# Attention of batches three to eight in quarters of TensorE's array, with a new layout of the PSUM banks

## The chip, the core and the metric

One core of a Trainium2 chip runs the whole program. TensorE (PE) multiplies and writes its products to PSUM, eight banks of 512 fp32 columns on 128 partitions; VectorE (DVE), ScalarE (ACT) and GpSimd (POOL) do the elementwise work, SyncE (SP) issues nearly all DMAs. PE keeps one operand in the array (a weight load, PEld in the profile) and streams the other through it, column by column. The metric is the device time of one execution in microseconds.

## What is computed

Eight batches of eight heads, 576 positions, 64 numbers per head. The first four heads attend to the last 32 positions ("plain"), the other four to every fourth of the last 128 ("dilated"). The heads' outputs, side by side, are the 512 columns of 4608 tokens, which go through a feed-forward of width 2048 with a leaky ReLU. Inputs and output are fp32, the kernel works in fp16.

```python
scores = scale * np.matmul(q, k.transpose(0, 1, 3, 2))
mask_plain = (rel >= 0) & (rel < window)                                       # window = 32
mask_dil = (rel >= 0) & (rel < window * dilation) & (rel % dilation == 0)      # dilation = 4
scores = np.where(masks[None, :, :, :], scores, -1000000000.0)
attn = np.exp(scores - np.max(scores, axis=-1, keepdims=True))
attn = attn / (np.sum(attn, axis=-1, keepdims=True) + 1e-09)
attn_out = np.matmul(attn, v)
x = attn_out.transpose(0, 2, 1, 3).reshape(B * S, H * D)
h = x @ w_in
return np.maximum(0.01 * h, h) @ w_out
```

## The kernel before

**Attention.** A visit is one pair of heads of one batch, four visits a batch in the order `VISITS` (2 and 3 dilated, 0 and 1 plain). `load_qk`, `load_v` and `load_rest` stage fp32 rows, `cast` turns them into fp16, `turn` puts Q and K of the pair into a slot with the 64 numbers of each head on partitions. For batches 0 and 1 (`b < EARLY`, `by_pe`) PE transposes; for batches 2 to 7 the load itself scatters 32-row pieces of 128 bytes (L437) and DVE transposes 32 by 32 (L708 to L720), with copies by POOL and ACT for the dilated order and for K, in which the keys of the two heads interleave, so that a full 128-row array holds 64 keys of each.

`unit` does half the queries of a visit: five score matmuls (L899) into one bank, Exp on ACT (L907), the product with a 0/1 table on DVE (L911; batches 0 and 1 add a bias on PE instead), row sums with a matrix of ones (L924), values (L918) into a second bank, Ln and Exp(−x) on ACT (L943, L945) for the reciprocal, and the product into `xt` on DVE (L956). For the plain visits from batch 2 on (`ADDED`; the 9 for the dilated ones means never) DVE or POOL first adds overlapping pieces of the weights (L932), which shortens the sums on PE.

**Feed-forward.** Twelve chunks of 384 tokens, three for two batches. `up` (L1057) multiplies `xt` by `w_in`, 16 blocks of four matmuls of 384 columns, and ACT applies the leaky ReLU into `gt` (L1073); chunk 1 is done in halves (`up_pair`, L1091). The last three chunks use seven products instead of eight (`ups7`, L1191). `down` (L1271) and `group` (L1361, seven products for four tiles) multiply by `w_out`; ACT and DVE evict, SP stores.

**What sets the order.** Every piece of work is a task of `_Plan` with its engine, a duration that the planner assumes, and what it waits for. `_Plan.run` makes a list schedule eight times and takes the best; the table `NUDGE` then shifts the priority of single tasks by their number, `HAND` fixes the engine of some, and the plan is made once more. The instructions of each engine stand in that order for good. `WHEN` gives the due time of each batch's attention. Before the feed-forward starts, spare time of PE is filled with matmuls on zeros (L1475, L1601).

**Banks.** Eight separate tiles: `tp`, `ops` twice, `hps` twice (for `up`), `sps`, `fps` twice. Units use `sps` and `ops`; `group` uses `fps` and `tp`.

## Time and profile before

| | us |
|---|---|
| three runs | 293.78, 294.69, 296.07 |
| median | 294.69 |
| span of the profiled execution, first to last instruction | 292.5 |

The profiled execution's own time is not listed apart from its span; the median lies 2.2 us above the span. The engines' times in 40 equal slices of the span, in tenths, with the granted clock of TensorE and the DMA share:

```profile
PE   6899999999999999999999999999999999999995
PEld 2567776776787788677777877887688999999985
DVE  7877588674799789858839889897878889678672
ACT  3997987589869966878888987888767966755522
POOL 5420452458537746964873774653425000000000
PEclk9999999999999999999999999999999999999999
DMA  7999999799898959999799798751101210121133
```

Attention of the last batch ends in slice 33 (235 us); behind it only the last chunks are left. The page's groups by line stand with the prediction, where they are used.

### The profile page before, as it was taken

What the parts mean: (1) busy time and instruction counts of PE and PEld (TensorE: products, weight loads), DVE (VectorE), ACT (ScalarE), POOL (GpSimd) and SP (SyncE); (2) the same over time, 40 slices, a digit from 0 to 9 for tenths busy, and PEclk for the clock granted to TensorE, in tenths of its full rate; (3) what the DMA queues carried; (4) which work ended last, traced back from release to release, by engine and by line L of the source; (5) the groups of instructions that cost most, each with busy time, mean ns of one, the idle gap of its engine ahead of it and who ended that gap; (6) DMA issues with size and microseconds to landing.
All of it is one profiled execution on the core that took longest, in us unless ns stands there. A gap on an engine that the chain in (4) does not pass through costs nothing.

```text
span 292.5 us, 7626 instructions
## 1 busy us (share of the span) xinstructions
PE 285.2 (97%) x2924; PEld 226.4 (77%) x2924; DVE 226.8 (78%) x437; ACT 218.9 (75%) x483; POOL 121.2 (41%) x173
## 2 busy tenths in 40 slices
PE   6899999999999999999999999999999999999995
PEld 2567776776787788677777877887688999999985
DVE  7877588674799789858839889897878889678672
ACT  3997987589869966878888987888767966755522
POOL 5420452458537746964873774653425000000000
PEclk9999999999999999999999999999999999999999
DMA  7999999799898959999799798751101210121133
GB/s 244 267 389 396 395 377 224 150 168 218 142 188 185 179 144 174 191 168 208 197 170 160 180 205 151 195 134 59 36 2 36 75 38 0 38 74 36 38 109 110
DMA packets 156068, 47.15 MB, mean 161 GB/s; under 512 B 136832, under 2 KB 153344, under 8 KB 156032
## 3 DMA queue, kind: packets, MB, share of 16 engines
q1 hardware_dynamic: 155344, 46.04, 65.0%
q10 hardware_dynamic: 688, 0.63, 0.6%
q8 instruction: 23, 0.38, 0.5%
q14 instruction: 13, 0.11, 0.1%
HBM read 37.22 MB, written 9.44 MB: 160 GB/s over the span
## 4 chain that ended last, share of the span: by engine, by line
PE 93%; ACT 2%; DVE 2%; DMA 1%; issue 1%; ACTq 0%; DVEq 0%
PE hps L1057 27%; PE fps L1361 23%; PE tp L1361 9%; PE hps L1191 5%; PE fps L1271 4%; PE hps L1091 4%; PE ops L1191 3%; PE ops L918 3%; PE ops L899 2%; PE sps L899 2%; PE ops L924 2%; PE sps L1191 1%; DMA con<-consts 1%; PE sps L924 1%; PE ops L1361 1%; PE sps L918 1%
## 5 line engine op out<-in xcount | busy, mean ns | idle before, releaser
L1057 PE MATMUL hps<-xt,w_in 128*128 128x384 f16 x488 | 94.7, 325 | 0.0
L1361 PEld LDWEIGHTS <-gt 128*128 128x128 f16 x768 | 73.0, 98 | 9.8 <-DVE gt L1347 0.2
L1073 ACT ACTIVATE gt<-hps 128x384 f16<-128x384 f32 x122 | 59.1, 487 | 13.7 <-PE hps L1057 12.7
L1057 PEld LDWEIGHTS <-w_in 128*128 128x128 f16 x512 | 44.9, 98 | 21.3 <-issue 0.3
L505 POOL CAST slots<-vst 128x576 f16<-128x576 f32 x55 | 46.0, 861 | 22.7 <-DMA vst<-in_v_dram 5.6
L505 POOL CAST nat<-stg 128x576 f16<-128x576 f32 (+1 forms) x52 | 34.6, 687 | 48.6 <-DVE gt L1347 15.1
L1361 PE MATMUL fps<-w_out,gt 128*128 128x256 f16 x368 | 46.7, 272 | 0.0
L911 DVE TENSOR_TENSOR ee<-ee,con 128x384 f16<-128x384 f16 (+1 forms) x48 | 20.6, 430 | 15.3 <-ACT ee L907 14.9
L945 ACT ACTIVATE rc<-rc 128x288 f32<-128x288 f32 (+1 forms) x64 | 27.2, 436 | 1.1
L956 DVE TENSOR_TENSOR xt<-ops,rc 128x288 f16<-128x288 f32 (+2 forms) x44 | 19.3, 445 | 9.7 <-ACT rc L945 4.9
L516 ACT COPY slots<-turned 64x512 f16<-64x512 f16 (+1 forms) x30 | 23.8, 799 | 0.8 <-DVE turned L708 0.5
L1214 ACT ACTIVATE gt<-vst 128x384 f16<-128x384 f32 (+1 forms) x24 | 16.0, 684 | 8.0 <-DVE vst L1210 8.0
L899 PEld LDWEIGHTS <-slots 128*128 128x128 f16 x308 | 18.1, 98 | 4.7 <-DVE slots L517 0.4
L517 POOL COPY slots<-turned 64x576 f16<-64x576 f16 (+2 forms) x25 | 16.7, 675 | 11.2 <-ACT slots L516 3.5
L907 ACT ACTIVATE ee<-ops 128x416 f16<-128x416 f32 (+2 forms) x35 | 16.7, 487 | 3.6 <-PE ops L899 3.0
L918 PEld LDWEIGHTS <-slots 128*128 128x128 f16 x308 | 17.1, 97 | 2.8 <-ACT slots L504 0.6
L924 PEld LDWEIGHTS <-con 128*128 128x128 f16 x168 | 14.0, 97 | 5.9 <-issue 0.8
L708 DVE STREAM_TRANSPOSE turned<-nat 128x576 f16<-128x576 f16 x24 | 18.0, 759 | 0.1
L1390 ACT COPY stg<-fps 128x512 f32<-128x512 f32 (+1 forms) x20 | 10.4, 519 | 9.4 <-PE fps L1361 9.1
L907 ACT ACTIVATE ee<-sps 128x416 f16<-128x416 f32 (+2 forms) x29 | 14.4, 495 | 3.8 <-PE sps L899 2.7
L1347 DVE TENSOR_TENSOR gt<-gt 128x1024 f16<-128x1024 f16 x21 | 16.6, 789 | 0.3 <-PE fps L1361 0.2
L1191 PEld LDWEIGHTS <-w_in 128*128 128x128 f16 x192 | 16.2, 98 | 0.2
(158 smaller groups left out, 559.8 us busy)
## 6 DMA issues: line engine op xcount, KB each, us to landing
out_dram<-osb SPq DMA_DIRECT2D x32, 256.0 KB, 2.6
stg<-in_k_dram SPq DMA_DIRECT2D x48, 144.0 KB, 3.6
stg<-in_q_dram SPq DMA_DIRECT2D x48, 144.0 KB, 3.4
vst<-in_v_dram SPq DMA_DIRECT2D x16, 288.0 KB, 4.3
vst<-in_v_dram SPq DMA_DIRECT2D x32, 128.0 KB, 3.2
gt<-in_moe_w_in_dram SPq DMA_DIRECT2D x6, 512.0 KB, 6.8
stg<-in_q_dram SPq DMA_DIRECT2D x3, 512.0 KB, 6.9
stg<-in_k_dram SPq DMA_DIRECT2D x3, 512.0 KB, 9.1
```

Of the source, the lines that this page charges most:

```text
L505: return ENG[e].tensor_copy(out=dst, in_=src)
L516: return nc.scalar.copy(out=dst, in_=src)
L899: nc.tensor.matmul(p_bank[:, c:c + w], slot(tn, KB + 128 * s, 0, 128, [1, 128]), slot(tn, qx, 0, 128, *qd), start=first or not by_pe, stop ...
L907: lambda e: nc.scalar.activation(out=et[:, 0:n], in_=p_bank[:, 0:n], func=AF.Exp, scale=SCALE), prio)
L911: lambda e: nc.vector.tensor_tensor(out=et[:, 0:n], in0=et[:, 0:n], in1=con[:, table:table + n], op=ALU.mult), prio,
L918: nc.tensor.matmul(at(dst, 0, 128, o, *od), lhs(s), et[:, c:c + w], start=i == 0, stop=i == len(steps) - 1, skip_group_check=True)
L924: nc.tensor.matmul(at(p_bank, 0, 128, o, *od), block_ones, at(et, 0, 128, c, *cd), start=i == 0, stop=i == len(rows) - 1, skip_group_check ...
L945: lambda e: nc.scalar.activation(out=rt, in_=rt, func=AF.Exp, scale=-1.0), prio)
L1057: nc.tensor.matmul(ht[:, 0:n], at(w_in, 0, 128, vi * DFF + j // 2 * 256 + j % 2, [2, 128]), at(xt[m % 2], 0, 128, vi * 1152 + x0 + x, [1, n]),
L1073: lambda e: nc.scalar.activation(out=gt[c % NG][:, j * n_c + x:j * n_c + x + n], in_=ht[:, 0:n], func=AF.Prelu, alpha=0.01),
L1191: nc.tensor.matmul(bk[:, n * i:n * i + n], w(v, 2 * z + i), x(v), start=first and i == 0 and v == 0, stop=i == 1 and v == 1, skip_group_ch ...
L1361: nc.tensor.matmul(bk[:, x:x + HN], tl[:, off + j * step:off + j * step + 128], rhs(j), start=first and x == 0 and j == 0, stop=j == HJ - ...
```

## The change

It rewrites the attention of batches 2 to 7; batches 0 and 1 and the feed-forward keep their arithmetic.

- **Quarters.** A visit is done in one burst (`burst`). Each matmul has 64 rows and 64 columns of the array (`tile_position`): the row half p holds one half of the keys, the column half q one head. Scores: five blocks for each p and q, 20 matmuls. Sums (with a 64-column block of ones) 20, values 24 (plain) or 28 (dilated). A burst has the sums and values of an earlier visit (`now`) and the scores of the next one (`then`): 26 bursts, 24 of them with scores and 24 with sums and values. The row halves write different banks; a burst holds four banks, `lent` (the one of `fps0`, `fps1`, `tp32` that `group` uses last), `sps`, `ops0`, `ops1`, or, where `fps1` is lent, `ops1`, `ops0`, `fps1`, `sps`.
- **Banks in one tile** `psum`, in the order tp, fps0, ops0, sps, ops1, fps1, hps0, hps1. One instruction of ACT or DVE reads two banks that lie side by side: Exp of 2 × 448 or 2 × 384 columns, Ln of 2 × 288, the product into `xt`. Where the two are not neighbours (`far`), it stays two instructions.
- **Masks.** The bias on PE stays for batches 0 and 1. The table has 640 columns and a block of ones, in all 704 constants behind the bias instead of 1,600. The added overlaps (`ADDED`, `LAPS`) are gone.
- **Q, K, V.** For batches 3 to 7 DVE transposes straight into the slot; only the dilated order needs one more copy (POOL or ACT) for each of Q and K. Batch 2 (`b < PACKED`) is loaded in rows of 1 KB and transposed by PE, as batches 0 and 1. V from batch 2 on is loaded per head, in pieces of 512 or 256 bytes, and cast once a visit. The columns of V and the rows of `w_in` are laid out head after head, also for batches 0 and 1.
- **Order.** `place` sets a burst after every 4.65 blocks of `up` from the 20.5th on, which ends attention with chunk 8. `FIRST`, `NUDGE` and `HAND` are new throughout.

```diff
-WHEN = (3.92, 2.82, 39.64, 80.18, 115.4, 117.81, 161.72, 152.03)
+WHEN = (3.92, 2.82)
+PLACE = 20.5
+PACE = 4.65
+SWITCH = 0.3
...
-ADDED = (2, 9)
-LAPS = ("DVE", "POOL")
...
-    EARLY = 2
+    EARLY, PACKED = 2, 3
...
-    ee = [sbuf(f"ee{i}", [128, 544]) for i in range(NE)]
-    rc = [sbuf(f"rc{i}", [128, 320], FP32) for i in range(NR)]
+    e_all = sbuf("ee", [128, 896 * NV])
+    ee = [e_all[:, 544 * i:544 * i + 544] for i in range(NE)]
+    r_all = sbuf("rc", [128, 1152], FP32)
+    rc = [r_all[:, 320 * i:320 * i + 320] for i in range(NR)]
...
-    tpb = bank("tp", FP16)
-    tp32 = tpb.bitcast(FP32)
-    ops = [bank(f"ops{i}") for i in range(2)]
-    hps = [bank(f"hps{i}") for i in range(2)]
-    sps = bank("sps0")
-    fps = [bank(f"fps{i}") for i in range(2)]
+    psum = ps.tile([128, 4096], FP32, name="psum")
+    tp32, fps0, ops0, sps, ops1, fps1, hps0, hps1 = (psum[:, 512 * i:512 * i + 512] for i in range(8))
+    tpb, hps, fps, ops = tp32.bitcast(FP16), [hps0, hps1], [fps0, fps1], [ops0, ops1]
...
-        early, first = b < EARLY, b == 0
+        early, first = b < PACKED, b == 0
...
+        if b >= PACKED:
             got = []
+            for o, x in ((0, 0), (1, KB)):
+                if not dil:
+                    got.append(add("DVE", 0.72, [c_qk[o]] + old,
+                                   lambda e, o=o, x=x: nc.vector.transpose(
+                                       slot(tn, x, 0, 128, [1, S]), na[:, o * S:o * S + S]), prio))
+                    n_users.append(got[-1])
+                    continue
...
+        if b >= EARLY:
+            got = []
+            for o in range(2):
+                if not dil:
+                    dst = slot(tn, KB * o, 0, 128, [4, 128], [1, 4])
+                    src = at(bq, 0, 128, 512 * o, [1, 128], [128, 4])
+                else:
+                    dst = slot(tn, KB * o, 0, 128, [128 if o else 144, 4], [1, 128])
+                    src = at(bq, 0, 128, 512 * o, [128, 4], [1, 128])
+                got.append(move(dst, src, 512, after_q + old, prio, ("DVE", "ACT"), dil, bank_q))
...
-        t_m = t_e if by_pe else add(
-            "DVE", 0.08 + n * 0.00052, [t_e, t_con[0]],
-            lambda e: nc.vector.tensor_tensor(out=et[:, 0:n], in0=et[:, 0:n],
-                                              in1=con[:, table:table + n], op=ALU.mult), prio,
-            lock=True)
-
...
-        if added:
-            c0, d0, c1, d1, w = lap
...
+    def places(b, vi):
+
+        if vi < 2:
+            order = [(4, 0, 64)] + [(i, 64 + 96 * i, 96) for i in range(4)]
+            return [(i, c, w, [([1, 64], 64 * (i + 4 * p)) for p in range(2)],
+                     [([[1, w]], 64 * (i + 4 * p)) for p in range(2)]) for i, c, w in order]
+        got = []
...
+    def quarter(rows, cols):
+        return 64 * rows, 64 * rows + 64, 64 * cols, 64 * cols + 64
...
+    def burst(now, then, prio, lent):
+
+        seats = [ops1, ops0, fps1, sps] if lent is fps1 else [lent, sps, ops0, ops1]
+        room, mine, far = {}, {}, seats[2].offset - seats[0].offset > 512
+        for bk in seats:
+            room[key(bk)], mine[key(bk)] = grab(bk)
...
+        def product(bk, x, od, lhs, rhs, p, q, first, last):
+            p0, p1, q0, q1 = quarter(p, q)
+            jobs.append(lambda: nc.tensor.matmul(
+                at(bk, q0, q1, x, *od), lhs(p0, p1, q), rhs(p0, p1), start=first, stop=last,
+                skip_group_check=True, tile_position=(p0, q0)))
...
+            for n, two in enumerate(list(zip(sums_of(vi, 0), sums_of(vi, 1)))
+                                    + list(zip(values_of(vi, 0), values_of(vi, 1)))):
+                for p, (blk, c, w, dims, x, *part) in enumerate(two):
+                    if not part:
...
+        if then is not None:
+            b2, v2, en2, e_old, e2_users = then
+            t2 = slot_of[b2, v2]
+            for _, c, w, keys, asks in places(b2, v2):
+                for p in range(2):
...
+        t_b = add("PE", SWITCH + cols / 2400.0, deps, pe, prio, 0.0, "B")
...
+            t_l = add("ACT", 0.07 + S / 1200.0, [t_b] + r_old,
+                      lambda e: nc.scalar.activation(out=at(rt, 0, 128, 0, [288, 2], [1, 288]),
+                                                     in_=bass.AP(
+                                                         tensor=psum.tensor, offset=seats[1].offset + 224,
+                                                         ap=[list(psum.ap[0]), [
+                                                             seats[3].offset - seats[1].offset, 2], [1, 288]]),
+                                                     func=AF.Ln), prio)
+            t_r = add("ACT", 0.105 + S / 1200.0, [t_l],
+                      lambda e: nc.scalar.activation(out=rt, in_=rt, func=AF.Exp, scale=-1.0), prio)
...
+            for i, n0, n1 in ((0, 0, 32), (1, 32, 144)) if vi >= 2 else ((0, 0, 64), (1, 64, 288)):
+                w = n1 - n0
+                for p, np in [(0, 1), (1, 1)] if far and not i else [(0, 2)]:
...
+        for p, np in [(0, 1), (1, 1)] if far else [(0, 2)]:
...
+            done.append(add("ACT", 0.07 + np * n / 1200.0, [t_b] + e_old,
+                            lambda e, p=p, np=np, part=part: nc.scalar.activation(
+                                out=at(et, 0, 128, 448 * p, [448, np], [1, n]), in_=part,
+                                func=AF.Exp, scale=SCALE), prio))
...
+        t_m = add("DVE", 0.08 + 2 * n * 0.00052, done + [t_con[0]],
+                  lambda e: nc.vector.tensor_tensor(
+                      out=at(et, 0, 128, 0, [448, 2], [1, n]), in0=at(et, 0, 128, 0, [448, 2], [1, n]),
+                      in1=at(con, 0, 128, table, [0, 2], [1, n]), op=ALU.mult), prio, lock=True)
...
+    pairs, due = [], []
+    for b, vi in [(b, vi) for b in range(EARLY, B) for vi in VISITS] + [(B, None)] * 2:
+        pairs.append((due.pop(0) if due else None, (b, vi) if b < B else None))
+        if b < PACKED:
+            due.append((b, vi))
+        elif b < B and vi % 2:
+            due += [(b, vi - 1), (b, vi)]
...
+    def place(k):
+        return PLACE + PACE * k
+
+    def bursts(upto, prio):
+        while flow[0] < len(pairs) and place(flow[0]) <= upto:
+            now, then = pairs[flow[0]]
+            if then is not None:
+                b, vi = then
...
+            burst(now, then, prio, lent[0])
...
+            if c > 1:
+                bursts(n_up[0], begins[c] + j * 1.3)
...
-        if e >= EARLY:
-            fetch(e, WHEN[e], (WHEN[e + 1] - WHEN[e]) / 4)
-        attend(e, WHEN[e], (WHEN[e + 1] - WHEN[e]) / 4 if e else 1.0)
-        if m:
-            fetch(o, WHEN[o], 6.5)
...
+        for c, batches in ((3 * m, [e]), (3 * m + 1, [e, o]), (3 * m + 2, [o])):
+            if c in SEVEN:
+                if c == SEVEN[0]:
+                    bursts(1e9, begins[c])
+                    in_sums()
```

On PE, before: the five scores of one unit of a dilated visit, between two blocks of `up` (`hps` are up's banks, `ops` a unit's, `slots` Q and K).

```order
L1057 MATMUL hps_102<-xt_86,w_in 128x384
L899 LDWEIGHTS slots
L899 MATMUL ops_101<-slots 128x96
L899 LDWEIGHTS slots
L899 MATMUL ops_101<-slots 128x96
L899 LDWEIGHTS slots
L899 MATMUL ops_101<-slots 128x80
L899 LDWEIGHTS slots
L899 MATMUL ops_101<-slots 128x80
L899 LDWEIGHTS slots
L899 MATMUL ops_101<-slots 128x32
L1057 LDWEIGHTS w_in
```

On PE now: the middle of a burst, where the sums (`con` holds the ones, `ee` the weights) give way to the values (`slots` holds V).

```order
L1260 LDWEIGHTS con
L1260 MATMUL psum<-ee,con 64x32
L1260 LDWEIGHTS con
L1260 MATMUL psum<-ee,con 64x64
L1260 LDWEIGHTS con
L1260 MATMUL psum<-ee,con 64x64
L1260 LDWEIGHTS slots
L1260 MATMUL psum<-ee,slots 64x64
```

Scores, sums and values of a unit stood in three places among the feed-forward's blocks; now all 64 or 68 matmuls of a burst stand in one, 64 rows wide, each with its weight load.

On SP, before: the loads of batch 2 behind the constants (`stg` stages Q and K, `vst` V).

```order
L489 DMA con<-consts 128x1600
L489 DMA stg_65<-in_k_dram 32x36x32 x3
L489 DMA stg_64<-in_q_dram 32x36x32 x3
L489 DMA stg_65<-in_k_dram 32x36x32
L489 DMA stg_64<-in_q_dram 32x36x32
L489 DMA vst_73<-in_v_dram 64x2x64
```

On SP now, at the same place:

```order
L659 DMA con<-consts 128x704
L659 DMA stg_68<-in_q_dram 64x8x64
L659 DMA stg_68<-in_k_dram 64x8x64
L659 DMA stg_65<-in_k_dram 128x4x256
L659 DMA vst_73<-in_v_dram 64x4x128 x3
L659 DMA vst_74<-in_v_dram 64x5x64 x3
L659 DMA stg_64<-in_q_dram 128x4x256
```

Batch 2's K and Q come in one load for four heads where eight loads of 32 × 36 pieces stood, V in more loads.

On ACT, before: one visit's Exp, Ln and Exp(−x), among the leaky ReLUs of `up` (L1073).

```order
L907 ACTIVATE ee_81<-sps_104 128x384
L1073 ACTIVATE gt_90<-hps_103 128x384
L1073 ACTIVATE gt_90<-hps_102 128x384
L907 ACTIVATE ee_82<-ops_101 128x384
L1073 ACTIVATE gt_90<-hps_103 128x384
L943 ACTIVATE rc_83<-sps_104 128x288
L1073 ACTIVATE gt_90<-hps_102 128x384
L945 ACTIVATE rc_83<-rc_83 128x288
```

On ACT now (L1405 is up's leaky ReLU):

```order
L1318 ACTIVATE rc<-psum 128x576
L1359 ACTIVATE ee<-psum 128x896
L1405 ACTIVATE gt_80<-psum 128x384 x2
L1325 ACTIVATE rc<-rc 128x576
L1405 ACTIVATE gt_80<-psum 128x384 x2
L1359 ACTIVATE ee<-psum 128x896
```

Three instructions a visit took the place of six, each about twice as wide.

439 lines of the change are left out of this document (273 added, 166 removed), and 311 rows, old and new, of the table NUDGE.

## The prediction

> **What bounds the kernel now.** I read the page's busy line and its chain of waits first, then a table of stretches, then the order of time on PE.
>
> ```profile
> span 292.5 us, 7626 instructions
> PE 285.2 (97%) x2924; PEld 226.4 (77%) x2924; DVE 226.8 (78%) x437; ACT 218.9 (75%) x483; POOL 121.2 (41%) x173
> ...
> PE 93%; ACT 2%; DVE 2%; DMA 1%; issue 1%; ACTq 0%; DVEq 0%
> ```
>
> TensorE is busy for 97% of the span and carries 93% of the chain that ends last. A busy PE could still hide holes, so the next view cuts the span into stretches (length, busy time of each engine, granted clock, DMA share, GB/s).
>
> ```profile
> 0.00:24.00 24.00, 19.96 (x214) 12.43 (x215) 19.09 (x37) 17.57 (x40) 9.04 (x18) 1.00 0.94 308
> 24.00:60.00 36.00, 35.70 (x383) 26.27 (x380) 26.17 (x55) 28.28 (x66) 12.62 (x18) 1.00 0.99 298
> 60.00:100.00 40.00, 39.95 (x389) 29.71 (x388) 30.66 (x59) 34.24 (x75) 25.95 (x38) 1.00 0.94 182
> 100.00:150.00 50.00, 50.00 (x497) 38.56 (x495) 37.98 (x76) 39.11 (x89) 34.54 (x50) 1.00 0.88 177
> 150.00:200.00 50.00, 50.00 (x511) 39.33 (x510) 43.62 (x81) 42.52 (x95) 28.24 (x40) 1.00 0.82 170
> 200.00:235.00 35.00, 35.00 (x378) 29.20 (x377) 27.56 (x52) 27.02 (x64) 10.79 (x11) 1.00 0.09 32
> 235.00:290.00 55.00, 54.55 (x567) 50.85 (x563) 41.72 (x82) 30.11 (x60) 0.00 (x0) 1.00 0.16 54
> ```
>
> From 24 to 235 us PE is idle for 0.35 us in all, at full clock. So in the stretch that the change touches (batches three to eight, numbered 2 to 7 in the code, from about 64 to 235 us) the time is the sum of what PE streams. What ACT, DVE and POOL save there is worth nothing by itself. What counts is how long PE needs for attention before and after, and whether a new wait appears. The second tight resource is DMA, with a share of 0.82 to 0.99 up to 200 us.
>
> **What is removed from PE.** The order of time on PE shows three kinds of attention groups between the blocks of the feed-forward: scores (L899), sums (L924) and values (L918). The columns are start, length and what ran; a length holds the drain of the last matmul, which overlaps the next row. The cost of a group is therefore the start of the next row minus its own start.
>
> ```profile
> 117.32 0.34 PE L899 MATMUL ops<-slots 128*128 128x96 f16 x5
> 117.50 0.81 PE L1057 MATMUL hps<-xt,w_in 128*128 128x384 f16 x4
> ...
> 119.02 0.34 PE L918 MATMUL sps<-ee,slots 128*128 128x96 f16 x5
> 119.21 1.46 PE L1057 MATMUL hps<-xt,w_in 128*128 128x384 f16 x8
> 120.50 0.33 PE L924 MATMUL ops<-ee,con 128*128 128x192 f16 x3
> 120.69 1.46 PE L1057 MATMUL hps<-xt,w_in 128*128 128x384 f16 x8
> ...
> 131.24 0.35 PE L899 MATMUL ops<-slots 128*128 128x96 f16 x5
> 131.44 1.46 PE L1057 MATMUL hps<-xt,w_in 128*128 128x384 f16 x8
> 132.74 0.35 PE L899 MATMUL sps<-slots 128*128 128x64 f16 x5
> 132.92 0.81 PE L1057 MATMUL hps<-xt,w_in 128*128 128x384 f16 x4
> ...
> 135.09 0.30 PE L924 MATMUL ops<-ee,con 128*128 128x32 f16 x3
> 135.23 0.65 PE L1057 MATMUL hps<-xt,w_in 128*128 128x384 f16 x3
> ```
>
> The six groups cost 0.18, 0.19, 0.19, 0.20, 0.18 and 0.14 us, on average 0.18. Six batches times four visits times two units are 48 units of three groups: 144 × 0.18 = **25.9 us removed**.
>
> **What is added to PE.** First, batch 2 is now transposed by PE as batches 0 and 1 are: four visits of eight transposes and four for the rest, 36 in all.
>
> ```profile
> 8.94 0.39 PE L791 MATMUL fps<-con,rest 128*128 128x128 f16 x4
> 9.16 0.22 PE L743 MATMUL fps<-con,nat 128*128 128x128 f16 x1
> ```
>
> Four cost 9.16 − 8.94 = 0.22, so 36 cost **2.0 us**.
>
> Second, the 26 bursts: 24 visits with scores and 24 with sums and values, in all 1,584 matmuls of 64 rows by 64 columns, each with a weight load of its own, where 612 full ones stood. No row shows a matmul in a quarter, so I bound it. The price of a full one follows from these rows (the third, from the chain of waits, is 16 matmuls of 192 columns):
>
> ```profile
> 21.74 0.53 PE L997 MATMUL sps<-slots 128*128 128x16 f16 x14
> 22.11 0.30 PE L924 MATMUL ops<-ee,con 128*128 128x192 f16 x3
> ...
> 27.26 1.32 PE hps L1091 x16
> ```
>
> A matmul of 192 columns costs 1.32/16 = 82.5 ns, one of 384 costs 1.29/8 = 161 ns (119.21 to 120.50), so about 0.41 ns a column and 3 ns a matmul; one of 16 columns costs 0.37/14 = 26 ns, a floor under the short ones, weight load included.
>
> Lower end: the four quarters run at once. Each streams 1,216 columns a visit (1,280 plain, 1,152 dilated) in 16.5 matmuls: 1,216 × 0.41 + 16.5 × 3 ns = 0.55 us, plus about four short ones raised to 26 ns (0.04), so 0.59 us × 24 = **14.2 us**, 9 ns a pair. Upper end: every pair waits its turn at the floor of 26 ns, 1,584 × 26 = 41.2 us. I take the lower end: the rows' cost runs with the columns streamed, and four quarters stream apart from each other.
>
> The page "TensorEngine Tiling (Array Packing)" of the Trainium skill, section Key Properties, says that different tiles load weights and multiply in parallel; no run here shows it yet.
>
> Third, the change of shape at a burst's two ends. No row shows one. The nearest is the drain that every group shows: the eight matmuls at 119.21 last 1.46 us, until 120.67, while the next begin at 120.50, so 0.17 us of each block drains under its successor. If shapes can't overlap, each of the 52 ends costs up to 0.17 us, 8.8 us in all; if they can, nothing. With no row nearer to either I take the middle, one drain a burst: 26 × 0.17 = **4.4 us**. The same section of that skill page says that changing the tiling mode drains the engine; by that the sum would take the full 8.8 us, and the time would be 293.8.
>
> **What is moved beside PE.** ACT and DVE work on both heads of a visit at once.
>
> ```profile
> L945 ACT ACTIVATE rc<-rc 128x288 f32<-128x288 f32 x48 | 20.7, 442 | 0.9
> L907 ACT ACTIVATE ee<-ops 128x384 f16<-128x384 f32 (+1 forms) x26 | 12.8, 502 | 3.3 <-PE ops L899 2.7 <-DVE turned L713 0.6
> L943 ACT ACTIVATE rc<-ops 128x288 f32<-128x288 f32 x26 | 10.4, 409 | 3.1 <-PE ops L924 3.1
> ```
>
> ACT gave a visit 2 × (502 + 409 + 442) = 2.71 us. With the slope between L943's 288 columns and L907's mean of 400 (about 0.85 ns a column) one Exp of 896 takes an estimated 0.92 us and the 576-wide Ln and Exp 0.65 and 0.69: 2.26 us, 0.45 less, 11 us over 24 visits. DVE loses one of two mask products, the added rows of L932 and the turned copies, POOL and ACT most copies out of them. All of it lies beside PE (hidden, worth 0); if that cover went, PE's own 0.35 us of idle time is all that it could have cost before.
>
> A burst waits once, for four banks, its masked weights, V and the next visit's Q and K; behind it on PE stands the whole feed-forward. The bursts stand some 3 to 13 us of PE work apart, and the chain from a burst's scores to the next one's weights is one Exp and one mask product, so I cost that wait at 0.
>
> DMA: batch 2's Q and K leave the 32-row, 128-byte pattern for 1 KB pieces; the constants shrink from 1,600 to 704 columns; V is cut into more pieces. The start (Q of group 0 first on SP, POOL's casts in another order) has 4.0 us of PE idle in its 24; I take no change there, give or take 1 us.
>
> **The sum.** −25.9 + 2.0 + 14.2 + 4.4 = −5.3 us. The profile's span, 292.5, lies 2.2 below the runs' median of 294.69, and that difference stays: **289.4 us**. Without any drain it is 285.0, with both drains 293.8.
>
> **The rivals.**
>
> *Quarters take turns* (slower). The whole gain hangs on one number: with drains as above the 1,584 pairs must cost less than (25.9 − 2.0 − 4.4)/1,584 = 12.3 ns each, about half the floor of 26. Two at a time: 28.4 instead of 14.2, 303.6 us. All in turn: 41.2, 316.4 us. For it speaks that no pair in the trace is faster than 26 ns; against it, that those all use the same full array.
>
> *Quarters' weights come too slowly* (no change). The loads' records here take 98 ns for 128 columns:
>
> ```profile
> L918 PEld LDWEIGHTS <-slots 128*128 128x128 f16 x308 | 17.1, 97 | 2.8 <-ACT slots L504 0.6 <-issue 0.5
> ```
>
> If half the columns took half of it, 49 ns, and the four loads of a step ran side by side without the next step's overlapping, 396 steps would cost 19.4 us instead of 14.2: 294.6 us. The skill's page "TensorE: Matmul & The Clock Gate", section LDWEIGHTS (loading the stationary operand), gives columns/1.2 ns, 53 ns for 64 (for 128 it gives 107, where the rows have 98), and the tiling page's Restrictions say that column tiling turns the fast weight load off; by these the time would be an estimated 296.2.
>
> *Both drains and a weight load unhidden at each end.* 52 × (0.17 + up to 0.098) us: 293.8 to 298.9 us.
>
> *DMA comes too late.* The new order pulls attention forward: the instructions ahead of batch 4's first scores in the two programs, counted at the prices above, come to some 106 us of PE work before and 90 now. They began here:
>
> ```profile
> 115.84 0.34 PE L899 MATMUL ops<-slots 128*128 128x96 f16 x5
> ```
>
> With DMA at 0.94 before that, data must come up to 16 us sooner; batch 2's relief (some 14,000 packets fewer for that batch, V's smaller pieces counted) gives only part of it. If 3 to 8 us stay uncovered: 292.4 to 297.4 us.
>
> **How the numbers follow.** A measurement of this kernel can tell about 1% from no change, 2.9 us. Four quarters at once with drains between none and both: 0.62 (0.50 below 291.7 us, 0.12 within 1%). Slow weights: 0.07, within. Unhidden ends: 0.08 (0.03 within, 0.05 slower). Late DMA: 0.07 (0.04 within, 0.03 slower). Two at a time: 0.09, slower; all in turn: 0.07, slower. So faster 0.50, same 0.26, slower 0.24. The range runs from 285.0 (no drain) to 299.0 (unhidden ends) and leaves out the turns, 0.16; the likeliest case's own is 285.0 to 293.8.
>
> **What would show it.** In the new profile the 64-wide matmuls must start 9 to 10 ns apart within a burst and a visit's burst must cost 0.6 us plus its ends; the gap from the last matmul before a burst to its first, and after it, gives the drain. PE must stay at 50.00 of 50.00 us in the middle stretches. Starts 13 ns or more apart, PE idle before L1260 released by DMA or POOL, or an evict of hps stuck behind the 896-wide Exp would make the prediction wrong.

## The result: slower, 307.2 us against 294.6

| | before | after |
|---|---|---|
| median, us | 294.55 | 307.16 |
| lowest, highest (four runs each) | 293.78, 296.07 | 306.08, 311.2 |
| span of the profiled execution | 292.5 | 304.7 |

The ratio is 1.0411, 95% interval 1.0364 to 1.0458. The forecast was 289.4 us, in a range of 285.0 to 299.0. One execution of the changed kernel, 311.2 us, fell into a slower state and is not in the ratio; the median of its other three, 306.5 us, is what the experiments are compared with.

The page of the changed kernel: span, PE's busy time, the main DMA queue (packets, MB, share of 16 engines' span) and the chain that ended last.

```profile
span 304.7 us, 9438 instructions
PE 285.9 (94%) x3929; PEld 219.7 (72%) x3929; DVE 212.2 (70%) x386; ACT 197.7 (65%) x401; POOL 90.1 (30%) x124
...
q1 hardware_dynamic: 146608, 46.60, 62.9%
...
PE 33%; DMA 26%; SPq 22%; DVE 7%; issue 5%; POOL 3%; ACT 3%; POOLq 0%; DVEq 0%
```

PE carried 93% of the chain before and carries 33% now; 48% are SP's issues and the DMAs behind them. The stretches (length, busy time of each engine, granted clock, DMA share, GB/s) say where:

```profile
0.00:24.00 24.00, 17.65 (x160) 11.39 (x161) 14.44 (x30) 14.17 (x33) 12.32 (x23) 1.00 0.88 280
24.00:60.00 36.00, 35.66 (x391) 25.63 (x390) 23.98 (x50) 27.50 (x69) 14.94 (x21) 1.00 1.05 316
60.00:100.00 40.00, 37.51 (x635) 25.69 (x633) 27.71 (x58) 30.20 (x64) 12.96 (x18) 1.00 0.83 172
100.00:150.00 50.00, 47.53 (x790) 35.02 (x788) 34.15 (x60) 32.84 (x62) 18.39 (x27) 1.00 0.88 164
150.00:200.00 50.00, 46.19 (x746) 33.87 (x747) 33.19 (x56) 33.58 (x62) 18.30 (x27) 1.00 0.83 172
```

PE was full between 60 and 200 us; now it idles there for 8.8 us, at full clock, and 2.3 us more than before in the first 24. No other engine filled up: over the whole span DVE, ACT and POOL are all less busy than before.

Two bursts in the order of time on PE, an undisturbed one and one that waits:

```profile
142.65 0.98 PE L1389 MATMUL psum<-xt,w_in 128*128 128x384 f16 x5
143.55 0.38 PE L1260 MATMUL psum<-ee,con 64*64 64x96 f16 x20
143.77 0.38 PE L1260 MATMUL psum<-ee,slots 64*64 64x64 f16 x24
143.98 0.35 PE L1260 MATMUL psum<-slots 64*64 64x96 f16 x20
144.27 1.48 PE L1389 MATMUL psum<-xt,w_in 128*128 128x384 f16 x8
...
160.29 0.38 PE L1260 MATMUL psum<-ee,con 64*64 64x96 f16 x20
162.69 0.40 PE L1260 MATMUL psum<-ee,slots 64*64 64x64 f16 x24 [2.01 <-POOL slots L675]
162.92 0.34 PE L1260 MATMUL psum<-slots 64*64 64x96 f16 x20
163.20 1.48 PE L1389 MATMUL psum<-xt,w_in 128*128 128x384 f16 x8
```

In the first, 64 quarter pairs start within 0.607 us, 9.5 ns a pair; the five full matmuls ahead cost 5 × 0.162 = 0.81 (0.162 us is the median from one start to the next at 384 columns), so the burst begins 0.09 us late, and 0.11 us pass from its last pair to the next full matmul. A whole burst costs 0.81 us. The second has the same 64 pairs and takes 2.91 us, since its values wait for POOL's cast of V. All of PE's waits from 60 to 240 us come to 8.4 us in eight rows (total, times, longest, by what ended them); the same view of the kernel before has no row. The three largest:

```profile
PE psum L1260 <- POOL slots L675: 3.4, 3, 2.0
PE psum L928 <- DVE xt L1342: 1.5, 2, 1.3
PE psum L1260 <- DVE xt L1342: 1.1, 1, 1.1
```

The cast of V is the largest of them, not the only one. Behind such waits stand loads: in that stretch POOL's casts of Q and K (`nat`) and of V (`slots`) waited 70.3 us for DMAs, against 4.4 before. The largest rows, three after and one before:

```profile
POOL nat L675 <- DMA stg<-in_q_dram: 23.2, 8, 7.4
POOL slots L675 <- DMA vst<-in_v_dram: 17.8, 6, 10.8
POOL nat L675 <- DMA stg<-in_k_dram: 14.1, 5, 8.3
...
POOL nat L505 <- DMA stg<-in_q_dram: 4.1, 1, 4.1
```

DVE's transposes (L900, L907) waited 15.4 us for POOL's casts in turn. The burst at 138.95 us shows how that reaches PE: it waited 1.1 us for DVE's product into `xt`, which stood in DVE's row behind a transpose that had waited 1.38 us for POOL's cast of K.

How the loads stand in SP's row shows in the chain of waits, here from 115 to 133 us (start, length, what):

```profile
115.60 0.39 SPq L659
116.04 0.60 SPq L659
116.68 0.64 SPq L659
117.36 3.70 DMA vst<-in_v_dram
...
125.47 1.40 POOL slots L675 x2
126.86 0.65 SPq L659
127.56 0.86 SPq L659
128.46 1.90 SPq L659
...
132.42 0.61 SPq L659
133.08 3.08 DMA stg<-in_k_dram
```

SP issues one DMA after the other, 0.6 us each where nothing holds it, and a load reaches its buffer 3 to 4 us after its turn. The rows of SP that start between 60 and 200 us add up to 130.2 us for 165 DMAs, 68 of them V, against 120.7 us for 146, 41 of them V, before. All loads of V by tile (duration min/median/max in ns, first and last start), before:

```profile
L489 SPq DMA_DIRECT2D vst<-in_v_dram x64: 601/608/2013, 4.1 to 190.2; - x64
```

and after:

```profile
L659 SPq DMA_DIRECT2D vst<-in_v_dram x104: 595/619/2558, 5.1 to 204.5; - x104
```

SP has 259 DMAs in place of 229. The DMA engines themselves have hardly more to do: 62.9% of 304.7 is 191.7 us of main-queue packet time. Before it was 190.1:

```profile
q1 hardware_dynamic: 155344, 46.04, 65.0%
```

**One number for PE's waits.** For each kernel I added up the work PE had done at each moment, from the trace's matmuls at their prices without waits (columns × 0.417 ns + 2.5, at least 26 ns, which fits the medians from one start to the next: 42, 82, 162 and 216 ns for 96, 192, 384 and 512 columns; a quarter of that for a quarter pair; 0.1 us for each end of a burst; the fillers on zeros count nothing). The time minus that work is how far PE is behind. Some 3 us behind the last matmul complete the span.

| us behind at | 24 | 60 | 100 | 150 | 200 | end | work in all |
|---|---|---|---|---|---|---|---|
| before | 13.7 | 14.3 | 14.7 | 14.7 | 14.6 | 14.8 | 274.6 |
| after | 16.5 | 17.1 | 21.6 | 25.3 | 30.1 | 30.9 | 270.5 |

So the work fell by 4.1 us, 2.8 were lost in the first 24 us, and 13.8 between 60 us and the end, where the kernel before lost 0.5.

### The profile page after: what moved, and what is told of

The parts are those of the page before. It is cut to its first block, busy times and chain, and to the rows that moved or that the text cites. A ratio compares the mean times of both kernels' runs of the same rounds, so it can differ in the third digit from the quotient of the medians.

```text
span 304.7 us, 9438 instructions
## 1 busy us (share of the span) xinstructions
PE 285.9 (94%) x3929; PEld 219.7 (72%) x3929; DVE 212.2 (70%) x386; ACT 197.7 (65%) x401; POOL 90.1 (30%) x124
## 3 DMA queue, kind: packets, MB, share of 16 engines
q1 hardware_dynamic: 146608, 46.60, 62.9%
## 4 chain that ended last, share of the span: by engine, by line
PE 33%; DMA 26%; SPq 22%; DVE 7%; issue 5%; POOL 3%; ACT 3%; POOLq 0%; DVEq 0%
SPq L659 22%; PE psum L1692 18%; PE psum L1522 9%; DMA stg<-in_k_dram 8%; DMA stg<-in_q_dram 7%; PE psum L1389 5%; DMA xt<-in_moe_w_out_dram 3%; DMA gt<-in_moe_w_in_dram 3%; DMA vst<-in_v_dram 3%; DMA wst<-in_moe_w_out_dram 2%; DVE xt L1342 2%; POOL nat L675 2%; DVE slots L907 1%; PE psum L1260 1%; ACT gt L1405 1%
## 5 line engine op out<-in xcount | busy, mean ns | idle before, releaser
L1389 PE MATMUL psum<-xt,w_in 128*128 128x384 f16 x512 | 98.1, 326 | 1.2 <-ACT gt L1405 1.1
L1405 ACT ACTIVATE gt<-psum 128x384 f16<-128x384 f32 x128 | 61.7, 493 | 30.7 <-PE psum L1389 28.3
L1692 PE MATMUL psum<-w_out,gt 128*128 128x256 f16 x512 | 64.1, 273 | 0.4 <-DVE osb L1729 0.3
L675 POOL CAST slots<-vst 128x640 f16<-128x640 f32 (+1 forms) x34 | 25.3, 769 | 44.3 <-DMA vst<-in_v_dram 21.1
L1342 DVE TENSOR_TENSOR xt<-psum,rc 128x448 f16<-128x448 f32 (+2 forms) x52 | 27.7, 592 | 7.5 <-ACT rc L1325 6.9
L1359 ACT ACTIVATE ee<-psum 128x896 f16<-128x896 f32 (+3 forms) x30 | 21.5, 724 | 7.2 <-PE psum L1260 7.2
L1541 DVE TENSOR_TENSOR vst<-psum,vst 128x384 f32<-128x384 f32 x36 | 19.3, 553 | 8.0 <-PE psum L1522 4.8
L1366 DVE TENSOR_TENSOR ee<-ee,con 128x768 f16<-128x768 f16 (+1 forms) x24 | 14.7, 612 | 14.4 <-ACT ee L1359 14.4
L907 DVE STREAM_TRANSPOSE slots<-nat 128x576 f16<-128x576 f16 (+2 forms) x30 | 15.2, 551 | 9.4 <-POOL nat L675 9.4
L900 DVE STREAM_TRANSPOSE slots<-nat 128x576 f16<-128x576 f16 x20 | 14.6, 757 | 6.0 <-POOL nat L675 6.0
L1325 ACT ACTIVATE rc<-rc 128x576 f32<-128x576 f32 x24 | 16.6, 692 | 0.2
L1522 PEld LDWEIGHTS <-w_in 128*128 128x128 f16 x192 | 16.5, 98 | 0.3
L1692 PE MATMUL psum<-wst,gt 128*128 128x256 f16 x128 | 16.3, 273 | 0.0
L1260 PEld LDWEIGHTS <-slots 64*64 64x64 f16 x1104 | 12.5, 108 | 5.1 <-POOL slots L675 4.0
L1522 PE MATMUL psum<-xt,w_in 128*128 128x192 f16 x144 | 16.0, 246 | 0.0
```

The source lines that it names most:

```text
L675: return ENG[e].tensor_copy(out=dst, in_=src)
L907: return add("DVE", dur, [c_qk[o]] + old, lambda e: nc.vector.transpose(slot(tn, dst, 0, 128, [1, n1 - n0]), na[:, o * S + n0:o * S + n1]) ...
L1325: lambda e: nc.scalar.activation(out=rt, in_=rt, func=AF.Exp, scale=-1.0), prio)
L1342: lambda e, args=args: nc.vector.tensor_tensor(out=args[0], in0=args[1], in1=args[2], op=ALU.mult), prio)
L1359: lambda e, p=p, np=np, part=part: nc.scalar.activation(out=at(et, 0, 128, 448 * p, [448, np], [1, n]), in_=part, func=AF.Exp, scale=SCALE ...
L1389: nc.tensor.matmul(ht[:, 0:n], at(w_in, 0, 128, vi * DFF + j // 2 * 256 + j % 2, [2, 128]), at(xt[m % 2], 0, 128, vi * 1152 + x0 + x, [1, n]),
```

## The experiments

Theories: **1**, SP's serial issue of more and smaller loads is the limit; **2**, the DMA engines' packets are; **3**, the fixed order asks for the loads too early; **4**, the order of the first loads costs the start. Several expectations count the changed kernel's V loads from batch four on; the pieces begin with batch three, so the edits of the changed kernel touched 36, 48 and 84 DMAs where the texts say 30, 40 and 70.

### Fewer, larger V loads

```diff
-                    lv += [load(queue, at(vs, p, p + 64, 320 * h, [D, 5], [1, D]),
-                                dram(v, base + h * HS + 256 * i * D, [D, 64], [64 * D, 5], [1, D]),
+                    lv += [load(queue, at(vs, p, p + 64, 0, [D, 32], [1, D]),
+                                dram(v, base + 256 * i * D, [D, 64], [64 * D, 32], [1, D]),
                                 320, 256, v_old, prio + 0.01 * h) for h in range(4)]
+                    once = [lv[-4].fn]
+                    for t in lv[-4:]:
+                        t.fn = lambda e, once=once: once and once.pop()(e)
...
```

> The changed kernel, in which each batch from the fourth on loads V of the plain heads with 2 DMAs (all 32 blocks that a half of the partitions needs, the gaps between heads included) instead of 8. That is 30 DMAs fewer on SP's queue and 7,680 packets of 256 B more; PE, DVE and ACT do the same work in the same order. Theory 1 (SP's serial issue, 0.62 us at least and 0.78 us on average each in 60 to 200 us, is what makes data late): 30 x 0.62 to 0.78 = 19 to 23 us of SP's time go, most of the 13.4 us that PE falls behind between 60 and 240 us comes back: 294 to 299 us against 307.2. Theory 2 (the DMA engines' packets are the limit, share 0.83 to 0.88): 7,680 packets x 21 ns / 16 engines = 10 us more of DMA work: 311 to 317 us. Theory 3 (the fixed order, which pulls attention forward, starves PE whatever the queue does): 305 to 309 us.

312.5 us, ratio 1.0599 (1.0537 to 1.0660): slower still, with 36 DMAs fewer on SP. The main DMA queue on its page:

```profile
q1 hardware_dynamic: 155248, 48.95, 68.7%
```

Packet time rose to 0.687 × 312.3 = 214.6 us, 23 more. The 9,216 packets added would make 10.3 us at their price in the changed kernel, 17.8 ns, but a packet of 256 B took longer here: 22.8 ns on average over the whole program (18.3 in the changed kernel), and 26.0 from 60 to 100 us. Fewer issues don't help if the engines get 23 us more to do. Theory 1 alone falls; theory 2 fits. The run does not separate packet time from a second effect: each large load also landed later, 7.1 us after its issue (median) where a small one took 2.9. No run takes the added V issues away at equal bytes and in SP's own row.

### Half the Q and K packets

```diff
+        half = ([32, 36],) if b == 3 else ([64, 18],)
...
-                lo = [load("SP", at(st, 32 * a, 32 * a + 32, 0, [32, 36], [1, 32]),
+                lo = [load("SP", at(st, 32 * a, 32 * a + 32, 0, *half, [1, 32]),
                            dram(src, base + (a // 2) * 2 * HS + (a % 2) * 32,
-                                [D, 32], [32 * D, 36], [1, 32]),
+                                [D, 32], [half[0][0] * D, half[0][1]], [1, 32]),
```

> The changed kernel with half of the packets of the Q and K loads of batches four to seven (indices 4 to 7): every second block of 32 tokens is not loaded, so these batches' attention is wrong. As many DMAs on SP's queue as before, 36,864 packets of 128 B fewer (of 147,339). Theory 1 (SP's serial issue): an issue takes as long for half the packets, so 304 to 309 us, as the changed kernel. Theory 2 (packets): 36,864 x 21 ns / 16 = 48 us less DMA work, so that the wait goes: 294 to 299 us. Theory 3 (the fixed order): 305 to 309 us. If SP's mean issue in 60 to 200 us falls well below 0.78 us, towards 0.62, the two limits are coupled and the time lies between.

298.5 us, ratio 1.0144 (1.0088 to 1.0200), with the same 259 DMAs on SP. Two of its stretches:

```profile
100.00:150.00 50.00, 50.00 (x821) 37.01 (x810) 35.74 (x63) 36.41 (x68) 21.82 (x31) 1.00 0.62 130
150.00:200.00 50.00, 50.00 (x794) 36.69 (x793) 38.45 (x61) 36.49 (x68) 21.61 (x28) 1.00 0.58 132
```

That is 8 us less than the changed kernel, inside what theory 2 had given. PE is full again from 100 to 200 us: the waits there are for loads. SP's mean issue over the whole program fell from 737 to 656 ns. The V loads, which the edit leaves alone, share in it: from 60 to 200 us their mean issue fell from 772 to 702 ns. So part of an issue is waiting for the engines to take packets: the two limits are coupled, as the last sentence of the expectation allowed.

### SP's first loads in the old order

```diff
+    first = [t for t in order if t.eng == "SP"][:6]
+    starts = [t.start for t in first]
+    for i, x in zip((4, 0, 5, 1, 2, 3), starts):
+        first[i].start = x
+    order.sort(key=lambda t: (t.start, t.n))
```

> The changed kernel with only SP's first six DMAs in another order: the two halves of Q of the first batch's dilated heads first and third, as the kernel before has them, ahead of the loads of plain heads and behind at most one load of the rest. Theory 4 (the start lost 2.7 us because that Q now goes fifth and sixth on SP): the first transposes come at 5.9 us instead of 7.5, and 1.5 to 3 us come back: 304.2 to 305.7 us. Theory 1 alone (all that matters is the stretch of 60 to 200 us, whose queue is not earlier for it): 306.5 to 307.5 us.

308.8 us, ratio 1.0458 (1.0411 to 1.0505): nothing gained, and the first transposes came at 8.82 us, later than 7.49. Theory 4 as I had put it falls.

### The kernel before with 30 more DMAs

```diff
+    if b >= 3:
+        lo.fn = lambda e, hh=hh: [nc.sync.dma_start(
+            every2(vs, hh, VH * hh + D * m, [D, n], [1, D]),
+            dram(v, base + 2 * hh * HS + 64 * D * m, [D, 64], [64 * D, n], [1, D]))
+            for m, n in ((0, 5), (5, 4), (9, 5), (14, 4))]
```

> The kernel before, in which each of the two V loads of the plain heads of batches four to eight is issued as 4 DMAs (5, 4, 5 and 4 blocks) in place of one: 30 DMAs more on SP's queue, the same packets and bytes, nothing else. Theory 1 (SP's serial issue): SP is busy 119.6 of 130 us in 60 to 190 us there; 30 x 0.62 = 18.6 us more, 10.4 us of them in its slack: 3 to 9 us slower, 298 to 304 us against 294.6. Theory 2 (packets) and theory 3 (the order of the attention): no change, 293.5 to 296 us.

302.4 us, ratio 1.0258 (1.0223 to 1.0294), inside the range of theory 1. Two stretches of it:

```profile
100.00:150.00 50.00, 47.43 (x464) 36.09 (x463) 39.24 (x74) 36.43 (x83) 31.77 (x45) 1.00 0.81 163
150.00:200.00 50.00, 46.88 (x480) 36.00 (x478) 38.17 (x75) 39.59 (x92) 29.63 (x42) 1.00 0.84 165
```

and its main DMA queue:

```profile
q1 hardware_dynamic: 155824, 46.04, 63.1%
```

The changed kernel's waits appear in the kernel before: the same bytes, 0.631 × 300.4 = 189.6 us of packet time against 190.1, nothing changed on PE, and PE waits 5.7 us in 100 to 200 us, at a DMA share of 0.81 and 0.84 where it was 0.88 and 0.82. Thirty more issues on SP cost 7.4 us. The share fell from 100 to 150 us while the loads came later: a falling DMA share is no sign of a relieved queue.

Theory 5 joins the two limits: a load's place in the stream costs the larger of its issue and its packets. No run measures that load by load.

### V loads on ACT's queue

```diff
+        t.act = lambda e: nc.scalar.dma_start(dst, src)
...
+            if not g:
+                for t in lv:
+                    t.fn = t.act
```

> The changed kernel with the 40 V loads of plain heads (8 a batch, batches four to eight) issued by ACT's queue instead of SP's, at the same places of the order; packets, bytes and DMA engines are the same. After the first four runs the theories are: T5 (coupled: a load's slot on SP is the larger of the 0.62 us that its issue takes and the time that its packets hold the engines, so Q and K loads cost about 1.0 us, V pieces 0.62, and small pieces cannot be hidden behind large ones): 40 x 0.62 = 25 us of SP's slots go, the loads become limited by the engines alone, 6 to 12 us come back: 295 to 301 us, minus what 40 issues of 0.55 us (the ACT issue at the start took 1.10 us for 2) cost on ACT. T2 (the engines' packets alone): as the changed kernel, 305 to 309 us, or slower for ACT's issues.

> As the run above with all 70 V loads of batches four to eight on ACT's queue. T5: SP's slots fall by 70 x 0.62 = 43 us, more than the lag needs; 294 to 300 us, or up to 3 us above the run above where ACT's 70 x 0.55 = 39 us of issues delay its evictions. T2: 305 to 309 us or slower.

324.0 us for 48 DMAs in the fastest of four executions (330.3 to 331.9 in the others) and 334.5 us for 84 (ratio 1.1361, 1.1305 to 1.1418), both far above what either theory gave (the second has `if True` for `if not g`). The first run from 100 to 150 us:

```profile
100.00:150.00 50.00, 43.43 (x675) 31.53 (x675) 30.10 (x48) 28.69 (x53) 14.34 (x19) 0.97 0.67 129
```

The DMA share is down to 0.67, and SP has no DMA row in 24 of these 50 us. ACT's loads stand in its row behind evictions, and ACT waited 51.5 us for PE between 60 and 200 us (36.2 in the changed kernel). PE in turn needs V, so I read this as a loop of waits; no run takes it apart. This tells nothing between theories 2 and 5.

### A new order, with the loads as slow as they are

```diff
-NUDGE = {
...
+NUDGE = {}
+HAND = {}
...
-        t = plan.dma(queue, 0.65, took(n, size) * (FSERVE if prio < -1400 else SERVE), deps,
+        t = plan.dma(queue, 0.8, took(n, size) * (FSERVE if prio < -1400 else SERVE), deps,
```

The first run has the empty tables alone.

> The changed kernel with both tables of numbers (the nudges of priorities and the engines chosen by hand) empty, so that the planner alone sets the order, with its 0.65 us for an issue. It is the base for the next run. T3 (the fixed order asks for the loads too early) and T5 both expect about the changed kernel's time: 302 to 310 us, since the order is still made for a queue that issues every 0.65 us.

> As the run above, with the planner's issue of a DMA at 0.80 us (the mean that SP's rows show from 60 to 200 us) in place of 0.65, so that attention is ordered for the loads as the chip serves them. T3 (the wait is a matter of order: other work of PE's could stand where it now waits): 296 to 301 us, and PE busy for 49.5 us or more of 50 in 100 to 200 us. T5 without T3 (the rate of the loads sets the end whatever the order): within 3 us of the run above.

308.9 us, ratio 1.0470 (1.0415 to 1.0525), as the changed kernel; and 303.1 us, ratio 1.0290 (1.0258 to 1.0323). An order made for slower loads is worth 5.8 us against the first run, with the same DMAs, and 3.4 against the changed kernel. The second run from 150 to 200 us:

```profile
150.00:200.00 50.00, 49.66 (x795) 36.39 (x793) 35.38 (x59) 34.76 (x66) 18.23 (x26) 1.00 0.79 155
```

From 60 us to the end PE falls behind by 7.9 us instead of 13.8. Theory 3 holds for part of it; 296 to 301 was too hopeful, since the stretch from 100 to 150 us still lost 4.3 us and the new order lost 4 us between 24 and 60.

### Batch four by PE's transposes too

```diff
-    EARLY, PACKED = 2, 3
+    EARLY, PACKED = 2, 4
...
+    rests = [rest, sbuf("rest3", [128, 512])]
...
```

> As the replanned run with 0.80 us for an issue (303.1 us), and batch four (index 3) takes the path of batch three: Q and K in 4 loads of 1,024 B rows and 2 for the rest instead of 16 loads of 128 B rows, turned by 36 PE transposes (2.0 us). On the loads that is 10 DMAs fewer, and 18,432 x 12.8 ns / 16 = 14.7 us of DMA work become 2,048 x 48 / 16 + 1,024 x 17.8 / 16 = 7.3 us. In all ten kernels so far the end comes 89 to 104 us after the last load of Q, K or V is issued. If the stream of loads sets the end: the last load comes some 7 us earlier than the 213.8 us of that run, and the time falls by 4 to 7 us, to 296 to 299 us, though PE has 2 us more to do. If PE's own work or the order sets it: 304 to 306 us.

> As the run above with 0.72 us for an issue in the planner, and the changed kernel's hand-made tables for its first 260 tasks, which are the start. If the stream of loads sets the end, and the replanned runs lost up to 3.3 us in 24 to 60 us because their start was planned without those tables: 293 to 297 us, PE busy for 35.5 us or more of 36 in 24 to 60 us. If not: 303 to 306 us.

301.5 us (1.0240, 1.0195 to 1.0284) and 302.6 us (1.0266, 1.0219 to 1.0313), both between the two ranges of their expectations. The stream did end 10.8 us earlier (last load issued at 203.0 instead of 213.8 us) and PE was nearly full, here in the first of the two:

```profile
100.00:150.00 50.00, 50.00 (x855) 36.52 (x856) 35.99 (x62) 37.87 (x71) 19.97 (x30) 1.00 0.85 162
150.00:200.00 50.00, 49.78 (x840) 37.09 (x829) 36.64 (x60) 34.59 (x65) 20.71 (x28) 1.00 0.78 161
```

but the span fell by 3.1 us only (PE is 5.7 us less behind at the end, with 2 us more work), and the medians by 1.6, with intervals of the ratio that overlap. The steady distance of the end from the last load, on which I had built, held only while the stream was the bound. In these two PE is 19.7 and 20.4 us behind at 60 us already (14.3 before).

### V loads on POOL's queue

The edit is ACT's, with `nc.gpsimd` in place of `nc.scalar`.

> The changed kernel with the 40 V loads of plain heads of batches four to eight issued by POOL's queue instead of SP's, at the same places of the order. POOL has the free time (busy 30%) and casts V itself, so it waits for no other engine there, as ACT did. No run shows what an issue costs on POOL. T5 (SP's slots and the engines together): 25 us of SP's slots go: 295 to 301 us if an issue on POOL costs 1 us or less. T2 (the engines' packets alone): 305 to 309 us. If POOL's issue is long (over 2 us), POOL's casts come late and it is slower, over 310 us, which would tell nothing of T5.

301.3 us, ratio 1.0227 (1.0175 to 1.0278), just above the 295 to 301 that theory 5 had given. Two stretches:

```profile
100.00:150.00 50.00, 49.88 (x855) 36.79 (x854) 37.05 (x63) 34.93 (x66) 28.47 (x42) 1.00 0.89 171
150.00:200.00 50.00, 48.88 (x787) 36.02 (x786) 36.10 (x60) 36.62 (x68) 32.86 (x48) 1.00 0.78 171
```

and its DMA queues, POOL's being q0:

```profile
q1 hardware_dynamic: 130480, 42.66, 59.3%
q0 software_dynamic: 2304, 3.94, 4.5%
```

48 DMAs leave SP, the packets' time is 178.2 + 13.5 = 191.7 us as in the changed kernel, and 5.2 us come back. With the 30 DMAs added to the kernel before, this shows from both sides that the number of issues in SP's one row costs time at equal DMA work, so theory 2 alone falls too and theory 5 is left. Here V also moved to a queue of its own; the 30 added DMAs, which stay in SP's row, are the test without that. The Trainium skill, "DMA: Bandwidth & Descriptors", section Rules for kernel authors, says that spreading DMAs over the issuing engines brings no bandwidth and only saves issue time; the trace agrees, with 191.7 us of packet time both times, and here the issue time was what counted.

> The changed kernel with all 70 V loads of batches four to eight on POOL's queue (the run before had 40 there, at 0.66 us each on POOL, and took 301.3 us). T5 (SP's slots and the engines together): SP loses 30 slots more, the DMA share in 60 to 200 us rises or the stream ends earlier than 199.0 us, 296 to 301 us; POOL has 70 x 0.66 = 46 us of issues beside 90 us of work. If the 40 were all that mattered, or POOL's issues now come in the way of its casts: 301 to 305 us.

308.9 us (1.0468, 1.0405 to 1.0532), above both ranges: the other 36 DMAs take it all back. POOL does everything in order, and its casts now stand behind issues, which I take for the cause: PE is 20.5 us behind at 60 us and 26.8 at 100, against 18.6 and 22.6 with 48, while SP has no DMA row in 9.1, 18.6 and 24.0 us of the three stretches from 60 to 200.

### The casts at the start

```diff
+    dve = [t for t in order if t.eng == "DVE" and t.kind == "cast"][:2]
+    dve[0].start, dve[1].start = dve[1].start, dve[0].start
+    act = [t for t in order if t.eng == "ACT" and t.kind != "dma"][:4]
+    for i in range(2):
+        act[i].start = act[3].start + 1e-4 * (i + 1)
+    order.sort(key=lambda t: (t.start, t.n))
```

> The changed kernel with only those four casts of the start in the other order. The stretch of 0 to 24 us gains the same 1.5 to 2.8 us, if theory 4b holds. If the stream of loads sets the end (in every run the end comes 89 to 105 us after the last load is issued), the gain is lost again behind it: 305.5 to 308 us. If the start adds to the waits of 60 to 200 us: 304 to 305.7 us.

> The run with 40 V loads on POOL's queue (301.3 us), with the order of four casts at the start changed: on DVE the cast of K that PE's first transposes need ahead of the cast of the rest, which waits for two loads of its own; on ACT the two casts of plain Q, which wait for a load of 512 KB, behind the two copies of K out of PSUM, for which PE's second transposes wait until 11.1 us. SP's order stays. PE is 2.8 us further behind at 24 us in the changed kernel than before. If those two waits make it (theory 4b): PE's first transposes at 6.9 us or earlier, the second near 9 us, and 1.5 to 2.8 us less: 298.5 to 300 us. If other loads of the start come in next: 300.5 to 302.5 us.

> The changed kernel with both edits of the start: SP's first six DMAs as in the kernel before, and the four casts in the other order. With the casts alone PE was 15.9 us of non-work behind at 24 us (16.5 in the changed kernel, 13.7 before), since its next wait, 1.47 us until 11.2 us, is for the Q that SP then sends fifth. If the two together are the start's loss: 14.2 us or less at 24 us, first transposes by 6.4, and PE's Q there by 9.7 us. The whole: 306 to 308 us if the stream of loads sets the end, 304 to 305.5 us if the start adds to it.

> As the run above with the 48 V loads of plain heads (8 a batch, six batches) on POOL's queue, which alone gave 301.3 us. If the stream of loads still sets the end: 301 to 303 us. If, with the stream relieved, the start adds to it: 297.5 to 300 us.

The first and third are 307.6 and 305.8 us (1.0474, 1.0425 to 1.0522; 1.0373, 1.0326 to 1.0421), which can't be told from the changed kernel; the two with 48 loads on POOL 302.8 and 302.7 us (1.0294, 1.0253 to 1.0334; 1.0277, 1.0221 to 1.0333), which can't be told from 301.3. The waits that I named went, in the first of them for instance: PE's first transposes came at 6.41 us in place of 7.49, the second at 8.59 in place of 11.14. But another stood behind each. With both edits of the start, a row from the order of time:

```profile
12.75 0.38 PE L928 MATMUL psum<-con,nat 128*128 128x128 f16 x4 [2.33 <-ACT slots L686]
```

PE is 15.8 to 16.3 us behind at 24 us in all four, not 13.7. So the cause of the start's loss is not found in one order; it stays open.

## Why the prediction was wrong

**Right: the quarters.** The lower end of the pair's price, 9 ns, was the right one: 9.1 to 9.7 ns in the undisturbed bursts, 0.607 to 0.612 us a burst against 0.59. Neither turns nor slow weights came about. The drain was near: 0.09 + 0.11 us for the two ends against one of 0.17, so 5.2 us against 4.4. That both ends cost something agrees with the Trainium skill, "TensorEngine Tiling (Array Packing)", section Key Properties, but each costs about 0.1 us, not the 0.17 that I would have charged by it. PE's work fell by 4.1 us where the sum had 5.3.

**The step that failed** is the sentence that costs a burst's wait at 0; in its place the runs showed 13.8 us lost after 60 us. Its reason looked only at the chain Exp, mask, next burst, which indeed hardly waits. The wait that came is for V, Q and K, named one sentence earlier, behind POOL's casts and DVE's transposes, behind loads. In "V is cut into more pieces" the sum had no term for 40 more issues of V, less the 10 of Q and K that batch three saves. The rows of SP, 0.6 us for each issue of a V load however small, were in the trace before and I didn't read them: I looked at the DMA share, in which SP's row doesn't appear.

**The rival that came true**, "DMA comes too late", had 0.07. Its mechanism was right, its price not: 3 to 8 us uncovered, against 13.8. It counted some 14,000 packets that batch three saves as relief; the whole queue has 8,736 fewer, since V's pieces are smaller in every later batch too, packet time didn't fall (191.7 against 190.1), and SP's row got longer. The pull forward was there: the program had put batch index 4's first scores some 16 us of PE work earlier; the burst that holds them began at 107.75 us, 8.1 us earlier than before, so about half of it was waited away.

**How much each part costs** the runs only bound: against the changed kernel's 306.5 us, relieving SP of 48 issues gives back 5.2 us, ordering attention for slower loads 3.4 (5.8 against the same planner with fast loads), half the Q and K packets 8.0. They act on the same waits and can't be added. The table of PE's delay, same columns as above:

| us behind at | 24 | 60 | 100 | 150 | 200 | end | work in all |
|---|---|---|---|---|---|---|---|
| before, 30 DMAs more | 14.0 | 14.5 | 15.0 | 18.1 | 22.0 | 22.1 | 274.6 |
| half Q and K packets | 17.4 | 18.1 | 20.9 | 21.3 | 21.8 | 22.3 | 270.5 |
| order for slower loads | 17.6 | 21.6 | 23.7 | 28.0 | 29.3 | 29.5 | 270.5 |
| 48 V loads on POOL | 17.6 | 18.6 | 22.6 | 23.4 | 25.2 | 26.6 | 270.5 |
| batch four by PE, slower loads | 17.7 | 19.7 | 22.4 | 22.9 | 23.6 | 23.8 | 272.5 |

Even with the loads most relieved (second and last row) PE ends 22.3 and 23.8 us behind, against 14.8 before: 3.7 and 4.0 us of the difference arise in the first 24 us, 2.5 and 3.7 between 24 and 100. In the first 24 us the executions of the four lower rows had a granted clock of 0.86, against 1.00 in the changed kernel's; the run with half the packets, whose start is the changed kernel's own, is 0.9 us further behind there, so some of that part may be the clock's. The rest is not explained. No version tried beats the kernel before.

**Start.** Taken at no change, give or take 1 us; it lost 2.8.

**What would show it wrong** was named rightly: PE idle ahead of L1260, released by POOL, is the row at 162.69. A third sign came once, and small: at 198.73 us `up` waited 0.90 us for an eviction of `hps` that stood on ACT behind a copy and a 768-wide Exp.

## What to carry to other kernels

Count the DMAs of the issuing engine as work of that engine, at the duration its rows show, before cutting a load into pieces: 30 more cost 7.4 us in a kernel whose work on PE, bytes and packet time stayed the same. Where one engine is full and the loads' stream nearly so, work taken off that engine can move the wait to the stream; here asking for the data sooner, with more loads, cost 13.8 us where 4.1 us of work were saved. When a queue is relieved by another engine, look at what that engine does in order: POOL took 48 issues well and 84 badly, ACT took even 48 badly.

## What the runs showed that I had not expected

- The issue of a V load takes 0.60 to 0.62 us on SP (least and median) and 0.67 on POOL, for 32 KB as for 288; other DMAs on SP go down to 0.31. With half of the Q and K packets the mean issue of the untouched V loads fell from 772 to 702 ns (60 to 200 us).
- On POOL's queue 15,360 packets of 256 B became packets of up to 4,096 B: the records count 2,304 packets for 48 loads, and 13.5 us of packet time.
- From 60 to 100 us packets of 256 B took 26.0 ns on average where V came in two large loads into 64 neighbouring partitions each, and 17.8 ns where it came in eight small ones. Why was not tried.
- The tile switch between 64 by 64 and the full array costs about 0.1 us at each end, and the four quarters of a step mostly start 3 to 4 ns apart.
